# Reordering three groups of transfers in the loading queue of stage one

## The chip, the cores and the metric

The kernel runs on one core of a Trainium2 chip. The core has four engines that compute, each with its own instruction stream: PE (TensorE, matrix products into PSUM), DVE (VectorE), ACT (ScalarE) and POOL (GpSimd). A fifth, SP (SyncE), computes nothing here: it is the queue that issues nearly all transfers (DMAs), in program order. ACT issues a few of its own. An instruction that waits holds up everything behind it on the same engine. The metric is the time of one execution in microseconds of device time; lower is better.

## The reference

For `x` of 2048 tokens by 448 channels, the result mixes an attention branch `a` and an MLP branch `b` with a gate:

```python
g = sigmoid((x * gate_w).sum(-1, keepdims=True))
q = (x @ wq) in 16 heads of 28;  k = x @ wk;  v = x @ wv     # one k and v for all heads
a = softmax(q k^T * 28**-0.5) v @ wo
h = gelu(layernorm(x) @ w1)
hs = concat(h[0:112] shifted +1, h[112:224] -1, h[224:336] +2, h[336:448] -2) @ w2   # shifts along tokens
x1 = x + hs
b = x1 + gelu(layernorm(x1) @ w3) @ w4
out = g * a + (1 - g) * b
```

All data are fp32. The kernel splits each fp32 operand into a high and a low part and adds the products of high with high, high with low and low with high.

## The kernel before, in words

The tokens are cut in four blocks of 512, each of four tiles of 128. The order of the instructions on every engine is written out by hand, so program order is the order of each queue.

Stage one (to about 127 us of the profile) computes the projections of `x` and the token-shift half of the MLP branch:

- `stage_q(u)` computes one of 16 units (block by head group) of queries, keys, values and gate; ACT copies the result out of PSUM (L297) and issues its own store to the DRAM buffer `qd` (L298).
- `stage_kv(b)` reads block b's values back from `qd` as rows of the tile `vT` (two DMAs, L329). `stage_v` later transposes `vT` on PE (L350).
- `stage_w1(b)` computes `h` for block b, token tiles on partitions; DVE transposes it in 32 by 32 squares into `ht` (L436), and four DMAs (L439) store it to the DRAM buffer `hd`. `read_h(b)` reads it back with channels on partitions into `hr` (two DMAs, L447), which has to wait until the four stores have landed. These are the block's "channels".
- `split_h(b)` makes the high part on ACT (L461) and the low part on POOL, or for block 3 half of it on DVE (L463); then `carry_h(b)` sends four small DMAs (L409, L410), once the low part of the third group is there.
- `stage_w2(b)` multiplies by `w2` (PE, L477, L478, L480), 11 products for each of four token tiles. The PSUM tile `hs` has two buffers, so PE can start tile t+2 only when DVE has added tile t into `x1` (L482).
- The normalised `x1` of block 0 is the input of the second MLP half. `layernorm_norm` makes it on DVE (L159, L160), `xt_write(0)` stores it to the DRAM buffer `xd` (four DMAs, L167), `xt_read(0)` reads it back transposed into `xr` (three DMAs, L172, L174) once those stores have landed, and `ln_split` makes high and low parts (ACT L633, DVE L636, L638).
- `load_w34(i)` loads a pair of `w3` and `w4` chunks (L607, L608); `split_w3` and `split_w4` split them (ACT L106 to L109 and L614, DVE L113, L114 and L617).

Stage two (to about 402 us) runs `w3` and `w4` over the four blocks. Stage three is attention and the output.

The end of stage one, with what hangs on what: DVE does, in this order, the additions of block 1, the low parts of `split_h(3)`, the additions of block 2, `ln_split` of chunks 0 and 1, the first addition of block 3, `ln_split` of chunks 2 and 3, the split of `w3` chunk 0, the second addition, the split of `w4` chunk 0, and so on:

```python
def third(t):
    if t == 3:
        ln_split(0, 0, 2)
stage_w2(NB - 2, third)
def weights(t):
    if t == 0:
        ln_split(0, 2, 4)
    if t % 2 == 0:
        split_w3(t // 2)
    else:
        split_w4(t // 2)
        load_w34(t // 2 + 1, s2a)
```

So a late `xr` holds DVE, and with it the additions that PE waits for.

The loading queue from block 2 on, before the change: carries of block 1, `read_h(2)`, carries of block 2, the stores of `h` of block 3, `xt_write(0)`, `read_h(3)`, `stage_kv(0..2)`, carries of block 3, `load_w34(0)`, `xt_read(0)`, `stage_kv(3)`.

Of the kernel before, what the change touches and what calls it, by code (L numbers as in the profile page):

```python
# [42 lines left out]
def gated_mix_kernel(  # L43
# [85 lines left out]
    def proj(ps, wh, wl, ah, al):  # L129
        for c in range(3):  # L130
            nc.tensor.matmul(ps, wh[:, c, :], ah[:, c, :], start=(c == 0), stop=False)  # L131
            nc.tensor.matmul(ps, wh[:, c, :], al[:, c, :], start=False, stop=False)  # L132
            nc.tensor.matmul(ps, wl[:, c, :], ah[:, c, :], start=False, stop=False)  # L133
        nc.tensor.matmul(ps, wh[:, 3, :], ah[:, 3, :], start=False, stop=False)  # L134
        nc.tensor.matmul(ps, wl[:, 3, :], ah[:, 3, :], start=False, stop=True)  # L135
# [28 lines left out]
    def xt_write(b, xt4):  # L164
        xd_of[b] = dram.tile([NE, 32, 4, 128], F32, tag="xd", bufs=2, name=f"xd_{b}")
        for p in range(4):
            nc.sync.dma_start(xd_of[b][:, :, p].rearrange("f i u -> i f u"),  # L167
                              xt4[32 * p:32 * p + 32].rearrange("i f t j -> i f (t j)"))

    def xt_read(b, raw):  # L170
        xd = xd_of.pop(b)
        nc.sync.dma_start(raw[:, 0:3, :], xd[0:12].rearrange("(c f) i p u -> (f i) c (p u)", c=3))  # L172
        for k in (0, 64):
            nc.sync.dma_start(raw[k:k + 64, 3, :], xd[12:14].rearrange("f i p u -> (f i) (p u)"))  # L174
# [75 lines left out]
    with tc.tile_pool(name="s1b", bufs=1) as s1b, \  # L250
# [5 lines left out]
        def mm1(name):  # L256
            k = turn[0] % 4
            turn[0] += 1
            return mm_tile(name) if k < 2 else ps1.tile([P, 512], F32, tag="tp", bufs=2, name=name)
# [34 lines left out]
        def q_out(u, ps):  # L294
            b, g = divmod(u, NG)
            qf = s1.tile([P, 512], F32, tag="qf", bufs=4, name=f"qf_{u}")
            nc.scalar.copy(qf, ps)  # L297
            nc.scalar.dma_start(qd[g, :, 512 * b:512 * b + 512], qf)  # L298
# [13 lines left out]
        def stage_q(u, tile_of=mm1):  # L312
            b, g = divmod(u, NG)
            ps = tile_of(f"q_{u}")
            w = slice(g * P, (g + 1) * P)
            proj(ps, wqh[:, :, w], wql[:, :, w], *xact[b])
            q_out(u, ps)
# [4 lines left out]
        def rest(g, n, b):  # L322
            cols = slice(512 * b, 512 * b + 512)
            return qd[g].rearrange("(j c) s -> j c s", c=32)[0:n // 4, DH:32, cols]

        def stage_kv(b):
            for g in range(2):
                at = 32 * b + 16 * g
                nc.sync.dma_start(vT[at:at + 16, :], rest(2 + g, 16, b))  # L329
# [84 lines left out]
        def token_tile(b):  # L414
            ht = s1.tile([P, 4, 512], F32, tag="raw", bufs=3, name=f"ht_{b}").rearrange("p c n -> p (c n)")
            return ht[:, 0:4 * D].rearrange("p (f t j) -> p f t j", f=NE, t=4)

        def stage_w1(b, between=None, ht=None):
            ah, al = xact[b]
            rs = rs1_of.pop(b)[1]  # L420
            if ht is None:
                ht = token_tile(b)
            for t in range(4):
                ps = mm1(f"h_{b}_{t}")[:, 0:D]
                tok = slice(t * P, (t + 1) * P)
                for c in range(3):
                    nc.tensor.matmul(ps, ah[:, c, tok], w1h[:, c, :], start=(c == 0), stop=False)  # L427
                    nc.tensor.matmul(ps, al[:, c, tok], w1h[:, c, :], start=False, stop=False)  # L428
                    nc.tensor.matmul(ps, ah[:, c, tok], w1l[:, c, :], start=False, stop=False)  # L429
                nc.tensor.matmul(ps, ah[:, 3, tok], w1h[:, 3, :], start=False, stop=False)  # L430
                nc.tensor.matmul(ps, ah[:, 3, tok], w1l[:, 3, :], start=False, stop=True)
                hf = s1.tile([P, 512], F32, tag="hf", bufs=3, name=f"hf_{b}_{t}")[:, 0:D]
                nc.scalar.activation(hf, ps, AF.Gelu_apprx_tanh, scale=rs[:, t:t + 1])
                if between:
                    between(t)
                nc.vector.transpose(ht[:, :, t, :], hf.rearrange("p (f j) -> p f j", j=32))  # L436
            hd = hd_of[b] = dram.tile([NE, 32, 4, 128], F32, tag="hd", bufs=2, name=f"hd_{b}")
            for p in range(4):
                nc.sync.dma_start(hd[:, :, p].rearrange("f i u -> i f u"),  # L439
                                  ht[32 * p:32 * p + 32].rearrange("i f t j -> i f (t j)"))  # L440

        def read_h(b):
            hd = hd_of.pop(b)
            hr_of[b] = s1.tile([P, 4, 512], F32, tag="raw", bufs=3, name=f"hr_{b}")
            rows = hd.rearrange("f i p u -> (f i) (p u)").rearrange("(m c) n -> c m n", c=C)
            for m0, m1 in ((2, 4), (0, 2)):
                nc.sync.dma_start(hr_of[b][0:C, m0:m1, :], rows[:, m0:m1, :])  # L447

        def split_h(b):
            hh[b] = s1b.tile([P, 4, 516], F32R, tag="hh", bufs=2, name=f"hh_{b}")  # L450
            hl[b] = s1b.tile([P, 4, 516], F32R, tag="hl", bufs=2, name=f"hl_{b}")
            hr = hr_of.pop(b)
            for tt in (hl, hh):
                if b == 0:
                    nc.gpsimd.memset(f32(tt[b])[0:C, :, 0:2], 0.0)
                else:
                    nc.gpsimd.tensor_copy(tt[b][0:C, :, 0:2], f32(tt[b - 1])[0:C, :, 512:514])
            for m in ORDER:
                raw = hr[0:C, m, :].rearrange("n (p t j) -> n p t j", p=4, t=4)
                hi, lo = [tt[b][0:C, m, 2:514].rearrange("n (t p j) -> n p t j", p=4, t=4) for tt in (hh, hl)]  # L460
                nc.scalar.copy(hi, raw)  # L461
                eng = nc.vector if b == NB - 1 and m in (0, 3) else nc.gpsimd
                eng.tensor_tensor(lo, raw, f32(hi), ALU.subtract)  # L463
                if m == 2:
                    carry_h(b)
            for tt in (hh, hl):
                if b:
                    nc.gpsimd.tensor_copy(tt[b - 1][0:C, :, 514:516], f32(tt[b])[0:C, :, 2:4])
                if b == NB - 1:
                    nc.gpsimd.memset(f32(tt[b])[0:C, :, 514:516], 0.0)  # L470
# [83 lines left out]
        stage_w1(2, lambda t: ln1_tile(3, t))  # L554
        split_h(1)
        read_h(2)
        stage_q(12)
        stage_q(13)
        mv0, rs0 = stats_tiles(s1, "m")
# [9 lines left out]
        h3 = token_tile(3)  # L569
        xt4 = token_tile("x")  # L570
        stage_w1(3, fourth, h3)
        xt_write(0, xt4)
        read_h(3)
        for b in range(3):
            stage_kv(b)
        stage_w2(1)
        split_h(3)
        stage_q(14)
# [16 lines left out]
        def big(name):  # L595
            return s2a.tile([P, 2048], F32, tag="big", bufs=2, name=name)

        def load_w34(i, pool):
            w3h.append(pool.tile([P, 4, 2 * P], F32R, name=f"w3h_{i}"))
            w3l.append(pool.tile([P, 4, 2 * P], F32R, name=f"w3l_{i}"))  # L600
            last = late if 2 * i + 2 == NF else pool
            w4h.append(last.tile([P, 2, D], F32R, name=f"w4h_{i}"))
            w4l.append(last.tile([P, 2, D], F32R, name=f"w4l_{i}"))
            raw = big(f"w34raw_{i}")
            raw3[i] = raw[:, 0:1024].rearrange("p (c n) -> p c n", c=4)
            raw4[i] = raw[:, 1024:1024 + 2 * D].rearrange("p (c n) -> p c n", c=2)
            nc.sync.dma_start(raw3[i], w3[:, :, i * 256:i * 256 + 256])  # L607
            nc.sync.dma_start(raw4[i], w4[i * 256:i * 256 + 256, :].rearrange("(c p) n -> p c n", p=P))  # L608
# [10 lines left out]
        acts, xraw2 = {}, {}  # L619
# [18 lines left out]
                    nc.vector.tensor_sub(hi[64:128], raw[64:128], f32(hi)[64:128])  # L638

        xraw2[0] = big("xr_0").rearrange("p (c n) -> p c n", c=4)  # L640
        load_w34(0, s2a)
        xt_read(0, xraw2[0])
        stage_kv(3)

        def third(t):
# [551 lines left out]
```

## Time and profile before

| | us |
|---|---|
| median of 3 runs | 914.38 (913.28 to 914.83) |
| the profiled execution | 915.15 |
| its span in the trace | 913.4 |
| PE busy | 903.0 |
| DVE / ACT / POOL busy | 544.1 / 632.8 / 105.5 |

The span is what the instructions cover; 1.75 us of the profiled execution lie around it. Times "at 104.6" below are microseconds from the start of the span. In the views, `PE hs L477` is an instruction of PE that writes the tile `hs` on line 477; `SPq` is SP issuing a DMA; `DMA hr<-hd` is a transfer from `hd` to `hr` on its way. The chain of waits is the chain of work that ended last, followed back from the last instruction; each piece has its start and its length. A windows view gives the busy time of the engines, the number of instructions, the granted clock of PE (1.00 is full), the share of the 16 DMA engines that was busy and what they moved in GB/s.

### The profile page before, as it was taken

The numbers are of one execution on the slowest core, as the hardware profiler recorded it, in microseconds if no ns is written. First come the engines' busy times: TensorE is split into PE (matmuls) and PEld (weight loads), VectorE is DVE, ScalarE is ACT, GpSimd is POOL, SyncE is SP. The second block draws the span as 40 slices with busy tenths as digits, with TensorE's granted clock in tenths as the row PEclk, the third lists the DMA queues.
The fourth block names the chain that finished last, engine by engine and source line by source line (L and its number), as shares of the span: only waits on it lengthen the run. The fifth ranks groups of instructions, "written<-read, shape, count | busy, mean of one in ns | idle before, by whom it ended". The sixth has DMA issues, their size and how long they took to land.

```text
span 913.4 us, 24127 instructions
## 1 busy us (share of the span) xinstructions
PE 903.0 (99%) x10097; PEld 648.0 (71%) x10097; DVE 544.1 (60%) x1085; ACT 632.8 (69%) x1135; POOL 105.5 (12%) x138
## 2 busy tenths in 40 slices
PE   9999899999999999999999999999999999999997
PEld 7899778888888888875565565565656556666654
DVE  4656263631435736546666666676666667666675
ACT  5443154431231222159999999999999999999995
POOL 3134100212000340002200000000000000000000
PEclk9999999999999999999999999999999999999999
DMA  9875754130122142120000001101011000010001
GB/s 305 309 174 137 206 164 130 24 84 21 26 74 52 24 105 66 27 65 24 26 25 4 26 14 48 31 26 26 3 46 46 26 3 26 14 55 14 15 14 43
DMA packets 50368, 58.23 MB, mean 64 GB/s; under 512 B 9376, under 2 KB 34768, under 8 KB 50256
## 3 DMA queue, kind: packets, MB, share of 16 engines
q1 hardware_dynamic: 47088, 50.95, 20.2%
q10 hardware_dynamic: 3168, 5.70, 1.8%
q8 instruction: 80, 1.31, 0.6%
q14 instruction: 32, 0.26, 0.1%
HBM read 39.80 MB, written 15.59 MB: 61 GB/s over the span
## 4 chain that ended last, share of the span: by engine, by line
PE 94%; DMA 2%; DVE 1%; SPq 1%; ACT 1%; issue 0%; POOL 0%; DVEq 0%; POOLq 0%; ACTq 0%
PE bank L995 24%; PE bank L958 22%; PE bank L859 8%; PE acc L709 5%; PE acc L708 5%; PE acc L710 5%; PE g L132 4%; PE g L131 4%; PE g L133 4%; PE g L134 1%; PE g L135 1%; DMA xr<-xd 1%; PE h L427 1%; PE h L428 1%; PE h L429 1%; PE q L309 1%
## 5 line engine op out<-in xcount | busy, mean ns | idle before, releaser
L985 ACT ACTIVATE p<-bank 128x512 f32<-128x512 f32 x762 | 386.9, 615 | 2.1 <-PE bank L958 2.0
L995 PE MATMUL bank<-p,vext 128*32 128x256 f32 x3076 | 244.4, 379 | 0.0
L995 PE MATMUL bank<-pd,vext 128*32 128x256 f32 x1020 | 241.1, 379 | 0.0
L982 DVE COPY pd<-bank 128x512 f32<-128x512 f32 x254 | 175.2, 691 | 50.8 <-PE bank L958 49.1
L995 PEld LDWEIGHTS bank<-p,vext 128*32 128x32 f32 x3076 | 126.4, 110 | 82.2 <-ACT p L985 0.5
L697 ACT ACTIVATE gh<-g 128x512 fp32r<-128x512 f32 x54 | 32.3, 599 | 182.0 <-PE g L135 182.0
L999 DVE TENSOR_TENSOR o<-o,bank 128x256 f32<-128x256 f32 x222 | 93.5, 421 | 92.2 <-ACT p L985 54.0
L990 ACT ACTIVATE pd<-pd 128x1024 f32<-128x1024 f32 x127 | 140.4, 1106 | 0.0
L958 PE MATMUL bank<-qh,kH 30*128 30x512 f32 x1024 | 118.0, 443 | 0.0
L995 PEld LDWEIGHTS bank<-pd,vext 128*32 128x32 f32 x1020 | 111.8, 110 | 0.1
L700 DVE TENSOR_TENSOR gl<-gf,gh 128x512 fp32r<-128x512 f32 x54 | 37.2, 688 | 118.1 <-ACT gf L698 118.1
L958 PE MATMUL bank<-qh,kL 28*128 28x512 f32 x1024 | 105.4, 392 | 0.0
L958 PE MATMUL bank<-ql,kH 28*128 28x512 f32 x1024 | 105.0, 391 | 0.0
L958 PEld LDWEIGHTS bank<-qh,kH 30*128 30x128 f32 x1024 | 60.9, 182 | 57.5 <-ACT p L985 46.0
L709 PE MATMUL acc<-w4l,gh 128*128 128x448 f32 x216 | 78.9, 365 | 0.0
L708 PE MATMUL acc<-w4h,gh 128*128 128x448 f32 x216 | 78.8, 365 | 0.0
L710 PE MATMUL acc<-w4h,gl 128*128 128x448 f32 x216 | 78.7, 364 | 0.0
L859 PE MATMUL bank<-wof,on 128*32 128x224 f32 x1008 | 73.1, 367 | 0.0
L132 PE MATMUL g<-al,w3h 128*128 128x512 f32 x168 | 65.8, 392 | 0.0
L131 PE MATMUL g<-ah,w3h 128*128 128x512 f32 x168 | 65.6, 391 | 0.0
L133 PE MATMUL g<-ah,w3l 128*128 128x512 f32 x168 | 65.5, 390 | 0.0
L958 PEld LDWEIGHTS bank<-ql,kH 28*128 28x128 f32 x1024 | 52.0, 185 | 8.8
(203 smaller groups left out, 1165.9 us busy)
## 6 DMA issues: line engine op xcount, KB each, us to landing
qd<-qf ACTq DMA_DIRECT2D x16, 256.0 KB
qm<-qd SPq DMA_DIRECT2D x16, 256.0 KB
qr<-qd SPq DMA_DIRECT2D x16, 256.0 KB
rb<-rd SPq DMA_DIRECT2D x15, 256.0 KB
x<-in_x_dram SPq DMA_DIRECT2D x4, 896.0 KB
hd<-ht SPq DMA_DIRECT2D x16, 224.0 KB
hr<-hd SPq DMA_DIRECT2D x8, 448.0 KB
w34raw<-in_w_dram SPq DMA_DIRECT2D x7, 512.0 KB
```

Source lines behind the costliest of these rows:

```text
L131: nc.tensor.matmul(ps, wh[:, c, :], ah[:, c, :], start=(c == 0), stop=False)
L132: nc.tensor.matmul(ps, wh[:, c, :], al[:, c, :], start=False, stop=False)
L133: nc.tensor.matmul(ps, wl[:, c, :], ah[:, c, :], start=False, stop=False)
L708: nc.tensor.matmul(ps, gh[:, tok], w4h[i][:, k, :], start=(f == 0), stop=False)
L709: nc.tensor.matmul(ps, gh[:, tok], w4l[i][:, k, :], start=False, stop=False)
L710: nc.tensor.matmul(ps, gl[:, tok], w4h[i][:, k, :], start=False, stop=(f == stop))
L859: nc.tensor.matmul(ps[32 * j:32 * j + 32, cols], on_of[u][:, tok], wof[:, u % NG, cols], start=start, stop=stop, tile_position=(0, 32 * j))
L958: nc.tensor.matmul(bs[j], w, a, start=(i == 0), stop=(i == 2), tile_position=(32 * j, 0))
L982: nc.vector.tensor_copy(ps[j], bs[j])
L985: behind[kt % 2] = nc.scalar.activation(ps[j], bs[j], AF.Exp, scale=SCALE)
L990: ins = nc.scalar.activation(pd, pd, AF.Exp, scale=SCALE)
L995: nc.tensor.matmul(pv[32 * j:32 * j + 32, q], vext[:, kt, :], p_of[u, kt][j][:, q], start=start, stop=stop, tile_position=(0, 32 * j))
```

## The change

Three groups of DMAs change their place in SP's queue. `stage_kv(0..2)` goes from behind `read_h(3)` to behind `read_h(2)`; `read_h(3)` goes ahead of `xt_write(0)`; `xt_read(0)` goes ahead of `load_w34(0)`. No DMA and no instruction of another engine is added, removed or altered.

```diff
         stage_w1(2, lambda t: ln1_tile(3, t))
         split_h(1)
         read_h(2)
+        for b in range(3):
+            stage_kv(b)
         stage_q(12)
         stage_q(13)
...
         h3 = token_tile(3)
         xt4 = token_tile("x")
         stage_w1(3, fourth, h3)
+        read_h(3)
         xt_write(0, xt4)
-        read_h(3)
-        for b in range(3):
-            stage_kv(b)
         stage_w2(1)
         split_h(3)
...
         xraw2[0] = big("xr_0").rearrange("p (c n) -> p c n", c=4)
+        xt_read(0, xraw2[0])
         load_w34(0, s2a)
-        xt_read(0, xraw2[0])
         stage_kv(3)
```

## The prediction

> **What bounds the kernel now.** I read the page first (busy times and the chain's shares), then the waits of PE, then windows around them, then the chain of waits.
>
> ```profile
> PE 903.0 (99%) x10097; PEld 648.0 (71%) x10097; DVE 544.1 (60%) x1085; ACT 632.8 (69%) x1135; POOL 105.5 (12%) x138
> PE 94%; DMA 2%; DVE 1%; SPq 1%; ACT 1%; issue 0%; POOL 0%; DVEq 0%; POOLq 0%; ACTq 0%
> ```
>
> PE is the bound nearly throughout. What can be won lies where the chain leaves PE, and PE's waits say where that is:
>
> ```profile
> PE hs L477 <- DVE x L482: 4.2, 2, 2.3
> ```
>
> Two waits, together 4.2 us: PE wants a buffer of `hs` that DVE has not yet added into `x1`. Seven windows of PE, cut at these gaps (length, PE busy and count, granted clock, DMA share, GB/s):
>
> ```profile
> 100.29:104.58 4.29, 4.29 (x22) 1.00 0.57 153
> 104.58:107.30 2.72, 0.37 (x3) 1.00 0.32 78
> 107.30:110.77 3.47, 3.47 (x9) 0.51 0.82 247
> 110.77:117.75 6.98, 6.98 (x35) 1.00 0.85 257
> 117.75:120.00 2.25, 0.38 (x3) 1.00 0.00 0
> 120.00:124.56 4.56, 4.56 (x16) 0.63 0.37 89
> 124.56:126.63 2.07, 2.07 (x11) 1.00 1.04 331
> ```
>
> These 26.34 us are `stage_w2(2)` and `stage_w2(3)`. The fourth window gives the undisturbed pace: 34 products in 6.98 us (the 35th was under way at its start), 0.205 each, so 2.27 for the 11 of a token tile. Eight tiles need 18.1 us, plus four transposes of `vT`, 0.80 at the low clock in the chain below, so about 0.4: 18.5 us. **7.8 us are lost**: 2.5 in the first gap, 1.6 at clock 0.51 behind it (3.47 less 9 x 0.205), 2.0 in the second gap, 1.7 behind that. This is the most that the change can win. What sets the gaps stands in the chain:
>
> ```profile
> 88.56 0.31 SPq L439
> ...
> 91.62 1.22 SPq L167
> ...
> 96.80 0.30 SPq L447
> ...
> 97.16 6.62 DMA hr<-hd
> ...
> 105.98 3.02 DMA qd<-qf
> ...
> 109.02 0.40 SPq L608
> ...
> 109.46 7.97 DMA xr<-xd
> ...
> 117.46 0.63 ACT ah L633
> ...
> 119.33 0.62 DVE x L482
> ...
> 123.72 0.80 PE vp L350 x4
> ```
>
> First gap: the stores of `h` of block 3 (88.56), then the stores of `xd` (91.62), only then `read_h(3)` (96.80), which takes 6.6 us; DVE's half of `split_h(3)` waits for it, and the additions of block 2 stand behind that. Second gap: `xt_read(0)` goes out at 109.46, behind both loads of `load_w34(0)`, and takes 8.0 us; ACT splits at 117.46, DVE adds at 119.33, PE resumes at 120.00.
>
> **The change part by part.** Nothing is added, so each part is a question of when. First the **values' rows**:
>
> ```profile
> 75.38 1.68 SPq L447 DMA_DIRECT2D hr<-hd  x2
> 82.03 0.56 SPq L409 DMA_DIRECT2D hh<-hl  x1
> 98.30 4.68 SPq L329 DMA_DIRECT2D vT<-qd  x6
> vT<-qd SPq DMA_DIRECT2D x8, 32.0 KB
> ```
>
> The six issues take 4.7 us. In their new place SP is free from 77.06 to 82.03, 5.0 us, so the carries of block 2 start on time. Nor does a delay there cost anything at once: those carries take four times about 0.6, and SP has nothing more to do before 88.56. The six read `qd` of blocks 0 to 2, stored long before. A loss is possible if their 192 KB slow `hr` of block 2, which lands at about 81.5 and feeds block 3's `h`; they stand behind it in the queue, so I take 0, with 0.5 us as the other end.
>
> **Channels of block 3.** `read_h(3)` now stands right behind its own stores and must wait for them to land. Block 0 has that pattern:
>
> ```profile
> 46.76 3.09 SPq L439 DMA_DIRECT2D hd<-ht  x4
> 53.18 0.81 SPq L447 DMA_DIRECT2D hr<-hd  x2
> 57.08 0.63 ACT L461 CAST hh<-hr 112x512 fp32r<-112x512 f32 x1 [2.05 <-DMA hr<-hd]
> 58.37 1.68 ACT L461 CAST hh<-hr 112x512 fp32r<-112x512 f32 x3 [0.67 <-DMA hr<-hd]
> 102.48 0.62 ACT L461 CAST hh<-hr 112x512 fp32r<-112x512 f32 x1 [15.48 <-PE hs L478]
> 103.80 1.67 ACT L461 CAST hh<-hr 112x512 fp32r<-112x512 f32 x3 [0.69 <-DMA hr<-hd]
> 106.64 1.14 DVE L482 TENSOR_TENSOR x<-x,hs 128x448 f32<-128x448 f32 x2
> ```
>
> The read went out 6.42 us after the first store (46.76 to 53.18): here 88.56 + 6.42 = 94.98, against 96.80. The issue gains only 1.8 us, since SP now sits out the landing. But the read no longer shares the engines with `xd`'s stores: its halves were used 3.90 and 5.19 us after the issue in block 0, 5.68 and 7.00 in block 3. So 98.9 and 100.2, each 3.6 us earlier. (The row names PE for the wait at 102.48, but `stage_w2(1)` was done by 95.2; it was the transfer.) DVE's additions move from 106.64 to 103.0. PE wants the buffer at 104.8: the **first gap goes**, with 1.8 us to spare, and its slow stretch with it: 4.1 us. As far as that, the end has not moved, because the second gap would take it all back: PE would reach it 4.1 us sooner and wait for the same `xr`. The sum hangs on the landing of `xr`.
>
> **MLP input.** The stores of `xd` now start behind `read_h(3)`, 94.98 + 1.45 = 96.4, and take 4.6 us to issue as before (91.62 to 96.20), to 101.0; the carries of block 3 follow, to 103.5. `xr` may be read when the stores have landed:
>
> ```profile
> 178.84 3.05 SPq L167 DMA_DIRECT2D xd<-xt  x4
> 185.22 0.38 SPq L172 DMA_DIRECT2D xr<-xd  x1
> 190.63 2.19 ACT L633 CAST ah<-xr 128x512 fp32r<-128x512 f32 x4 [0.84 <-DMA xr<-xd]
> qd<-qf ACTq DMA_DIRECT2D x16, 256.0 KB
> ```
>
> In block 1 the read went out 6.38 us after the first store and 3.33 after the last issue. So 101.0 + 3.3 = 104.3 is the early end, and 100.2 + 6.4 = 106.6 the late one (stores that move only when `hr` is in). I take the middle, 105.5, against 109.46. The closed pool's last reader of `hr` (DVE, just ahead of the row of 106.64) moves to 103.0 and doesn't hold it. Block 1's `xr` was used 5.41 us after its issue, in an empty queue; 7.97 here, behind two weight loads. I take 5.41 + 0.6 for the two query stores of ACT, which go out at 102.4 and 103.4 (105.98 and about one us later, less 3.6) and should land by 105.4 and 106.4: `xr` is used at **111.5** instead of 117.46. The late end adds the whole of those 512 KB at the 257 GB/s of the fourth window, 2.0 us.
>
> The Trainium skill ("DMA: Bandwidth & Descriptors", section "Issuing engines are not separate DMA queues") says that transfers of SP and ACT run on the same 16 engines and interleave; by it the two stores share time with `xr` to the last byte, and the 2.0 of the late end would be nearer than my 0.6, which makes the sum 1.4 us smaller. No row here separates the two queues.
>
> **Weights behind it.** What is late next?
>
> ```profile
> w34raw<-in_w_dram SPq DMA_DIRECT2D x7, 512.0 KB
> 121.29 0.60 SPq L607 DMA_DIRECT2D w34raw<-in_w_dram  x1
> 119.55 0.83 ACT L106 CAST w3h<-w34raw 128x768 fp32r<-128x768 f32 x1
> 125.60 0.84 ACT L106 CAST w3h<-w34raw 128x768 fp32r<-128x768 f32 x1 [3.53 <-DMA w34raw<-in_w_dram]
> 122.64 0.61 DVE L482 TENSOR_TENSOR x<-x,hs 128x448 f32<-128x448 f32 x1
> ```
>
> The first `w3` load goes out at 105.5 + 2.1 = 107.6, and behind `xr` its 512 KB need 1.6 us at the 331 GB/s of the last window: 113.1. ACT gets to it 2.09 after `xr` (117.46 to 119.55): 113.6. So the weights just hide, with 0.5 us; if they land later, each us is one on the second addition. PE without gaps starts the third tile of block 3 at 100.29 + 6 x 2.27 = 113.9 and the fourth at 116.55. The first addition allows the third tile 2.54 us after `xr` (117.46 to 120.00), at 114.0; the second one ends 5.79 after it (123.25), at 117.3. So PE waits 0.1 and then about 0.65 more: **0.75 us remain**. `stage_kv(3)` lands behind the weights, some 1.4 us after them by the same rate, before the transposes at 116.2. The second weight pair goes out when DVE is done with `xr` (121.29, 3.83 after it): 115.3, used 4.31 later at 119.6. The gelus behind that are then ready before PE needs the first PSUM buffer again, two gate tiles of 2.5 us into stage two. From there to the end PE sets the pace, so what stage one gains the end gains.
>
> **Sum:** 7.8 less 0.75 is 7.05 us. On the profiled execution: 915.15 - 7.05 = 908.1; it lay 0.8 over the median, so in the runs 914.38 - 7.05 = **907.3 us**.
>
> One cost has no row: whether a short gap drops the clock. Gaps of 2.72 and 2.25 us each cost 1.6 behind them; smaller ones up to 0.75 don't occur here. I take 0, the other end is 1.6. The Trainium skill ("TensorE: Matmul & The Clock Gate", "Part 1") says that the clock halves after a whole idle window of about 3.4 us. By that, neither gap could have slowed PE and the change would be worth only the 4.5 us of gaps less 0.75: 910.6. The windows speak against it (0.51 and 0.63 granted), so it has no chance of its own below; the slow stretches of about 3.4 us do fit its window's length.
>
> **The rivals.**
>
> *`xr` comes later* (stores at their late end, 106.6; the read 5.71 as the slowest later block might have it; 2.0 for the query stores): 114.3. The third tile then starts at 116.85 instead of 113.9, a gap of 3.0 us, which drops the clock as now: the fourth follows 4.2 us later as it does now (120.00 to 124.2), at 121.1 instead of 116.55, and 0.1 of the slow stretch is behind it. 7.8 less 4.65 leaves 3.15 us: **911.2**. For it: SP waits longer in two places, the same engines carry it all, and waits of SP for the query stores are already on the chain (3.02 before L608). Against: the DMA share is only 0.32 and 0.57 in the first two windows, so there is room. Chance 0.20.
>
> *Nothing gained*: `xr` is set by the bytes ahead of it, not by its place; the first gap goes and comes back as a longer second one. That needs `xr` at about 117, 11.5 us after its issue. **914.4**. Against it: 8.0 was the time with two weight loads ahead. Chance 0.11. That the order in the queue changes and nothing else comes of it would be this case too.
>
> *Slower*: the weights, now behind a read that itself waits for stores, become the bound. PE's fourth tile can't start before ACT's `w3` split begins plus 3.7 (119.55 to 123.25). It started at 124.2 before; a loss of 1.8 us needs the split to begin at 122.3, 14.7 us after the load's issue at 107.6, where 4.31 was needed in the row of 121.29. At 124 the end would be at **917.9**. Chance 0.05.
>
> **How the numbers follow.** Forecast, 906 to 909: 0.64. With the three rivals that is 1. A measurement of this kernel tells about 0.2%, 1.8 us, from no change. Faster: 0.64 + 0.20 = 0.84; same 0.11; slower 0.05. The range: from 906.6 (all 7.8 won) less 0.8 of the runs' spread, 905.8, to the late rival, 911.3.
>
> **What would show it.** Right: L447 of block 3 issued at about 95 and ahead of L167; ACT's L461 at 99 and 100; no PE wait near 104.8 and the clock at 1.00 there; `xr` issued ahead of L607, at 105 to 106, ACT L633 at 111 to 112; the gate products of stage two starting at about 119.6 instead of 126.6, and the rest shifted by as much. Wrong: the six L329 pushing L409 of block 2 beyond 83; L633 beyond 114; ACT waiting for `w34raw` ahead of its first L106; PE waiting for `vT`; or PE's later stages growing by what was won.

## The result, and the profile after

| | before | changed |
|---|---|---|
| median, us | 914.61 (4 runs, 913.28 to 915.74) | 907.82 (4 runs, 907.61 to 908.86) |
| ratio, 95% interval | | 0.9929 (0.9911 to 0.9946) |
| profiled execution / its span | 915.15 / 913.4 | 907.61 / 905.8 |

The change wins 6.8 us, 0.7%, by the medians (the two profiled executions are 7.5 us apart, since the changed one is the fastest of its four). The page of the changed kernel, PE's busy time and the chain that ended last by engine:

```profile
PE 899.7 (99%) x10097; PEld 644.9 (71%) x10097; DVE 543.4 (60%) x1085; ACT 632.9 (70%) x1135; POOL 105.8 (12%) x138
PE 99%; ACT 0%; DVE 0%; issue 0%; ACTq 0%; DVEq 0%
```

The chain had left PE for 6% of the span; now PE carries 99% of it. PE itself is busy 3.3 us less, with the same 10097 instructions: the slow stretches are gone. All waits of PE in the changed kernel (us in total, times, longest):

```profile
PE warm_ps L93 <- DVE warm L66: 1.1, 1, 1.1
PE bank L1131 <- DVE worst L1127: 0.4, 1, 0.4
PE bank L902 <- ACT p L985: 0.3, 1, 0.3
```

The row of `hs` on L477 is gone. The windows of PE around the end of stage one, first of the changed kernel, then the last stretch of the kernel before (length, PE busy and count, granted clock, DMA share, GB/s):

```profile
100.55:118.88 18.33, 18.33 (x93) 1.00 0.79 231
118.88:905.80 786.92, 781.87 (x9548) 1.00 0.14 39
```
```profile
126.63:913.40 786.77, 781.68 (x9548) 1.00 0.14 39
```

`stage_w2(2)` and `stage_w2(3)` take 18.33 us without a gap, where they took 26.34. The gate products start at 118.88 instead of 126.63, 7.75 us earlier, and what follows takes 786.9 us as before. So the whole difference lies ahead of stage two, and nothing of it is given back behind. What SP issued, from the timeline of the changed kernel (start, length, issue):

```profile
77.19 4.21 SPq L329 DMA_DIRECT2D vT<-qd  x6
82.09 0.63 SPq L409 DMA_DIRECT2D hh<-hl  x1
...
87.81 3.02 SPq L439 DMA_DIRECT2D hd<-ht  x4
94.25 0.81 SPq L447 DMA_DIRECT2D hr<-hd  x2
95.11 3.83 SPq L167 DMA_DIRECT2D xd<-ht_x  x4
100.27 0.59 SPq L409 DMA_DIRECT2D hh<-hl  x1
...
104.81 0.39 SPq L172 DMA_DIRECT2D xr<-xd  x1
105.91 1.14 SPq L174 DMA_DIRECT2D xr<-xd  x2
107.09 0.60 SPq L607 DMA_DIRECT2D w34raw<-in_w_dram  x1
```

and who used it (the idle time ahead and what ended it stand in brackets):

```profile
98.44 0.63 ACT L461 CAST hh<-hr 112x512 fp32r<-112x512 f32 x1 [11.33 <-DMA hr<-hd]
99.78 1.67 ACT L461 CAST hh<-hr 112x512 fp32r<-112x512 f32 x3 [0.72 <-DMA hr<-hd]
110.03 2.18 ACT L633 CAST ah<-xr 128x512 fp32r<-128x512 f32 x4 [7.05 <-DMA xr<-xd]
112.66 0.83 ACT L106 CAST w3h<-w34raw 128x768 fp32r<-128x768 f32 x1 [0.45 <-DVE x L482]
```
```profile
102.83 0.62 DVE L482 TENSOR_TENSOR x<-x,hs 128x448 f32<-128x448 f32 x1
115.22 0.60 DVE L482 TENSOR_TENSOR x<-x,hs 128x448 f32<-128x448 f32 x1
```

`hr` is used 4 us earlier than before, `xr` 7.4 us earlier (117.46 then). The second fence is DVE's timeline: it adds block 2's first tile at 102.83, when PE has just made it, and block 3's second at 115.22, before PE wants the buffer at about 116.5. Last, SP's own waits that bear on this (us in total, times, longest):

```profile
SPq L447 <- DMA hd<-ht: 3.2, 1, 3.2
...
SPq L172 <- DMA qd<-qf: 0.9, 1, 0.9
SPq L174 <- DMA qd<-qf: 0.7, 1, 0.7
```

The first is `read_h(3)` sitting out the landing of its own stores. The other two are odd: `xr` doesn't read `qd`. They turned out to matter.

### The profile page after: what moved, and what is told of

It is laid out like the page before. It is cut to its first block, busy times and chain, and to the rows that moved or that the text cites. A ratio compares the mean times of both kernels' runs of the same rounds, so it can differ in the third digit from the quotient of the medians.

```text
span 905.8 us, 24129 instructions
## 1 busy us (share of the span) xinstructions
PE 899.7 (99%) x10097; PEld 644.9 (71%) x10097; DVE 543.4 (60%) x1085; ACT 632.9 (70%) x1135; POOL 105.8 (12%) x138
## 4 chain that ended last, share of the span: by engine, by line
PE 99%; ACT 0%; DVE 0%; issue 0%; ACTq 0%; DVEq 0%
PE bank L995 24%; PE bank L958 23%; PE bank L859 8%; PE acc L709 5%; PE acc L708 5%; PE acc L710 5%; PE g L132 4%; PE g L131 4%; PE g L133 4%; PE hs L477 1%; PE hs L478 1%; PE g L134 1%; PE g L135 1%; PE hs L480 1%; PE h L429 1%; PE h L427 1%
```

## The experiments

The theory on trial: the two gaps are in series, and the end of stage one is set by the landing of `xr`. The rival: each of the three parts takes its own gap, independently. Three parts give eight kernels; with those before and after, six runs fill the table.

**The channels alone.**

```diff
         stage_w1(3, fourth, h3)
+        read_h(3)
         xt_write(0, xt4)
-        read_h(3)
         for b in range(3):
             stage_kv(b)
```

> Only read_h(3) goes ahead of xt_write(0); the values' rows and the order of xr and weights stay as before. Theory (two gaps in series, the end set by the landing of xr): the first gap goes, but the six L329 now stand between xd's stores and block 3's carries, so SP comes to load_w34(0) at about 106.6 and to xr at about 107.9; behind the weights xr takes 8.0 and ACT L633 starts at about 115.9. PE waits 4.5 us ahead of block 3's third tile and runs slow behind it: about 1.7 us faster than before, 912.9. Rival (two independent gaps, each part takes its own): 4.1 us faster, 910.5, with the second gap as long as before.

Measured: 917.32 (12 runs) against 914.81, ratio 1.0026 (1.0017 to 1.0034). It is *slower* than before, where both theories had a gain. From this run, in order: the timeline of SP, the waits of SP, the timeline of ACT, the waits of PE:

```profile
100.39 7.88 SPq L329 DMA_DIRECT2D vT<-qd  x6
108.39 0.63 SPq L409 DMA_DIRECT2D hh<-hl  x1
```
```profile
SPq L329 <- DMA qd<-qf: 2.9, 1, 2.9
```
```profile
118.94 2.18 ACT L633 CAST ah<-xr 128x512 fp32r<-128x512 f32 x4 [14.49 <-DMA xr<-xd]
```
```profile
PE hs L477 <- DVE x L482: 5.6, 1, 5.6
```

The first gap is gone: one wait on L477 is left. But the six rows take 7.9 us instead of the 4.7 they took before, since SP waits 2.9 us for a store of queries to land, which the rows of blocks 0 to 2 don't read. All behind them is late: the carries, the weights, and `xr`, used at 118.94, later than before. The second gap takes back all that the first gave, and more. PE also waits 0.6 and 0.2 us for the late carries near 111. That the second gap takes back the first holds; the forecast of 1.7 us gained was a miss in its sign too, since the theory knew nothing of that wait.

**The MLP input alone.**

```diff
+        xt_read(0, xraw2[0])
         load_w34(0, s2a)
-        xt_read(0, xraw2[0])
         stage_kv(3)
```

> Only xt_read(0) goes ahead of load_w34(0). Theory: the first gap stays (2.5 us and 1.6 us of low clock near 105 to 111), xr goes out at 107 to 109 and is used at 112.5 to 114.5, and PE, late by the first gap, finds DVE's additions done: no second gap, about 3.6 us faster than before, 911.0. Rival (independent gaps) gives the same 3.7 here; the two differ in e1.

Measured: 911.63 (6 runs), ratio 0.9961 (0.9947 to 0.9974). The time is as expected, and the one gap left is the first (`[1.90 <-DVE x L482]` on PE's L477 at 107.56). `xr` goes out at 107.68, as expected too, but is used 0.8 us after the latest time that I had given. It takes 7.65 us with no weight load ahead of it. What stands ahead of it are ACT's two query stores, by ACT's timeline:

```profile
106.23 0.34 ACTq L298 DMA_DIRECT2D qd<-qf  x1
...
107.28 0.34 ACTq L298 DMA_DIRECT2D qd<-qf  x1
115.33 2.19 ACT L633 CAST ah<-xr 128x512 fp32r<-128x512 f32 x4 [8.07 <-DMA xr<-xd]
```

**The values' rows alone.**

```diff
         read_h(2)
+        for b in range(3):
+            stage_kv(b)
...
         read_h(3)
-        for b in range(3):
-            stage_kv(b)
```

> Only the values' rows move. Theory: nothing waits for them, the carries of block 3 wait for POOL and not for SP, both gaps stay: within 0.3 us of before, 914.5. Rival (the six transfers are in the way of hr or xr by their traffic): up to 1 us faster. If they disturb block 2's channels in their new place: up to 0.5 us slower, L409 of block 2 issued after 82.5.

Measured: 915.07 (12 runs), ratio 1.0001 (0.9992 to 1.0009): nothing, as expected. L409 of block 2 went out at 82.33. PE's two waits are still there on its timeline:

```profile
106.51 0.47 PE L477 MATMUL hs<-w2h,hh 112*128 112x448 f32 x1 [1.20 <-DVE x L482]
119.94 0.74 PE L477 MATMUL hs<-w2h,hh 112*128 112x448 f32 x1 [4.12 <-DVE x L482]
```

This run shows the series most plainly. In its profiled execution the first gap is half as long as before (1.20 against 2.35), and the second has grown from 1.87 to 4.12, since `xr` is used at 117.41 as ever.

**Channels and input, rows left where they were.**

```diff
         stage_w1(3, fourth, h3)
+        read_h(3)
         xt_write(0, xt4)
-        read_h(3)
         for b in range(3):
             stage_kv(b)
...
+        xt_read(0, xraw2[0])
         load_w34(0, s2a)
-        xt_read(0, xraw2[0])
```

> The change without the move of the values' rows. Theory: both gaps shrink, but the six L329 hold SP until about 104, so block 3's carries and xr go out 2 to 3 us later than in the changed kernel (xr at about 106.6 instead of 104.8), L633 starts at about 112, the second addition of block 3 ends about 1.2 us too late for PE: about 6.5 us faster than before, 908.1 to 909, so the rows' move is worth 0.5 to 1.3 us here though it is worth nothing alone. Rival (the rows' move is worth nothing anywhere): 907.8, as the changed kernel.

Measured: 913.52 (12 runs), ratio 0.9979 (0.9968 to 0.9990). A miss: without the rows' move only 0.2% is left of the 0.7%. The same wait as in the first run is why (SP's timeline, then SP's waits):

```profile
99.45 7.84 SPq L329 DMA_DIRECT2D vT<-qd  x6
107.42 0.63 SPq L409 DMA_DIRECT2D hh<-hl  x1
...
110.14 0.52 SPq L172 DMA_DIRECT2D xr<-xd  x1
```
```profile
SPq L329 <- DMA qd<-qf: 3.1, 2, 2.8
```

The chain of waits has it too: `104.16 2.50 DMA qd<-qf`, then `106.67 0.63 SPq L329`. So `xr` goes out 5.3 us later than in the changed kernel (104.81).

In the program as compiled, the DMAs of SP and ACT take eight completion counters in turn, and each waits until the DMA that had its counter before it, eight earlier in the program's count, has landed. The two query stores of block 3 are issued by ACT behind `split_h(3)`, which itself waits for `hr`; with the channels moved, their counters fall to the fifth and sixth of the rows when these stand where they stood, and to the first two reads of `xr` in the changed kernel: the odd waits above. In the kernel before they fall to the second weight load and to the last read of `xr`, and SP's waits there show both:

```profile
SPq L608 <- DMA qd<-qf: 1.3, 1, 1.3
...
SPq L174 <- DMA qd<-qf: 0.6, 1, 0.6
```

The order of the counters is read off the program; the next run tries it.

**The same with the last two query stores issued by SP.**

```diff
-            nc.scalar.dma_start(qd[g, :, 512 * b:512 * b + 512], qf)
+            (nc.sync if u > 13 else nc.scalar).dma_start(qd[g, :, 512 * b:512 * b + 512], qf)
```

> As the run with channels and input alone (rows still between xd's stores and block 3's carries), but the last two query stores are issued by SP behind the carries instead of by ACT. Theory (a DMA must wait until the one eight before it in the program's count of DMAs, those of ACT included, has landed; so the sixth row waited for a query store): now the row's predecessor is a store of xd, landed by then, the wait of 2.8 us goes, and although SP issues two more DMAs, xr goes out at about 108 instead of 110.1: 1 to 3.5 us faster than that run, 910 to 912.3. Rival (the time is SP's issuing alone): 1.2 us slower than that run, about 914.7.

Measured: 912.12 (10 runs), ratio 0.9962 (0.9947 to 0.9977). The timelines of SP and of ACT:

```profile
99.86 4.19 SPq L329 DMA_DIRECT2D vT<-qd  x6
104.17 0.63 SPq L409 DMA_DIRECT2D hh<-hl  x1
...
107.98 0.39 SPq L172 DMA_DIRECT2D xr<-xd  x1
```
```profile
114.66 2.18 ACT L633 CAST ah<-xr 128x512 fp32r<-128x512 f32 x4 [11.35 <-DMA xr<-xd]
```

The rows take 4.2 us again, and `xr` goes out at 107.98 although SP issues two more DMAs. They read the same data as in the run before, and the wait of 2.8 us is gone, as the counters had it: it belongs to them and not to the data. In time it brings little: the query stores now stand in the same queue just ahead of `xr`, which is used 6.7 us after its issue (5.1 in the run before), so only 0.6 us of the 2.2 arrive. The intervals of the two runs overlap.

**The rows behind the weights**, the other way to take SP past that wait.

```diff
         xt_read(0, xraw2[0])
         load_w34(0, s2a)
+        for b in range(3):
+            stage_kv(b)
         stage_kv(3)
```

> The values' rows of all four blocks go behind load_w34(0) instead of ahead. Theory (what the move of the rows bought is that SP no longer stands between xd's stores and block 3's carries, where its sixth row waited 2.8 us for a query store): the late place is as good as the early one, xr at about 104.8 as in the changed kernel, PE waits at most 0.5 us for vT: 907.8 to 908.5. Rival (the early place itself matters, since the rows' traffic is then out of the way): 909 to 910.

Measured: 908.47 (6 runs), ratio 0.9923 (0.9909 to 0.9936), the changed kernel's value. So it is not the early place that pays: the late one, clear of the stretch between the stores of `xd` and block 3's carries as well, is worth the same. In its profile `xr` went out at 107.42 and not at 104.8, because the stores of `h` started late in it (90.36); counted from them it is 17.1 us, against 17.0 in the changed kernel. The price of the late place showed where it was expected, though longer, among the waits of PE:

```profile
PE vp L350 <- DMA vT<-qd: 1.6, 1, 1.6
```

**Channels and rows, weights still ahead of the input.**

```diff
         xraw2[0] = big("xr_0").rearrange("p (c n) -> p c n", c=4)
-        xt_read(0, xraw2[0])
         load_w34(0, s2a)
+        xt_read(0, xraw2[0])
```

(against the changed kernel)

> The change without its third part: read_h(3) ahead of xt_write(0), values' rows behind read_h(2), but load_w34(0) still ahead of xt_read(0). Theory: no first gap; SP reaches the weights at about 104.8 and xr at about 106.5, and behind the weights xr takes 6.5 to 8.0, so L633 starts at 113 to 114.5 and PE waits 1.6 to 3 us ahead of block 3's third tile: 910 to 911.6, half the gain. Rival (the weights ahead of xr cost nothing once SP is early): 907.8.

Measured: 913.52 (11 runs, 910.51 to 914.27), ratio 0.9972 (0.9960 to 0.9983). The profiled execution, at 911.53, is as expected: `xr` issued at 107.09, used at 114.06, one gap of 2.6 us. The median is 2 us worse than I had said. Ahead of the weights `xr` took 5.2 us in the changed kernel, behind them 7.0 here: both its place and its time in flight count.

**Rows and input, channels behind the stores of `xd`.**

```diff
+        xt_write(0, xt4)
         read_h(3)
-        xt_write(0, xt4)
```

(against the changed kernel)

> Rows and MLP input moved, channels of block 3 still behind xd's stores. Theory: the first gap stays (1.2 to 2.5 us, with the low clock behind it if it is over 1.6 or so), xr goes out at 107 to 108 and is used near 113 to 115, PE is late enough not to wait for it again: as the run with the input alone, 911 to 912. Rival (two of three parts bring two thirds): 910.

Measured: 912.18 (8 runs), ratio 0.9970 (0.9960 to 0.9981): as the run with the input alone, and as the theory had it. The first gap is there, 2.6 us at 107.78, and no second.

**The weights 1.45 us later.**

```diff
         xt_read(0, xraw2[0])
-        load_w34(0, s2a)
         stage_kv(3)
+        load_w34(0, s2a)
```

> The changed kernel with stage_kv(3) ahead of load_w34(0), so the first weights go out 1.45 us later. Theory: they had some 0.7 us to spare behind xr, so PE waits 0 to 0.5 us ahead of block 3's fourth tile, too short to lower the clock (a gap of 1.2 us in the run with the rows alone did not): 907.8 to 908.4. Rival (the weights set the end already): each us counts, 909.2.

Measured: 908.19 (6 runs), ratio 0.9919 (0.9905 to 0.9932); no loss that can be told. Its profiled execution is its slowest (910.05; the stores of `h` went out at 89.12 in it, 1.3 us after those in the changed kernel's profile) and shows two short gaps on PE's timeline:

```profile
114.82 0.47 PE L477 MATMUL hs<-w2h,hh 112*128 112x448 f32 x1 [0.65 <-DVE x L482]
118.50 0.47 PE L477 MATMUL hs<-w2h,hh 112*128 112x448 f32 x1 [0.72 <-DVE x L482]
```

**The changed kernel once more**, unaltered.

> The changed kernel once more, unaltered, for a second profiled execution. Theory: what is left over is thin. If the stores of h of block 3 start at 88.6 or later (they started at 87.81 in the first profile of it, at 88.6 to 90.4 in others), the weights or xr hold PE 0.3 to 1 us, without a drop of the clock; if they start before 88, not at all. Time 907.5 to 908.9 either way. Rival (the first profile is typical): no PE wait on L482 at all.

Measured: 908.52 (5 runs), ratio 0.9927 (0.9912 to 0.9942). The stores of `h` started at 88.76 in this profile, and PE did wait a little, by its timeline:

```profile
117.09 0.47 PE L477 MATMUL hs<-w2h,hh 112*128 112x448 f32 x1 [0.35 <-DVE x L482]
```

So the first profile, with no wait at all, was a favourable execution. The change leaves some tenths of a microsecond of slack, not more.

All eight together (ratio to the kernel before, measured beside each):

| | rows not moved | rows moved |
|---|---|---|
| nothing else | 1 | 1.0001 |
| channels | 1.0026 | 0.9972 |
| input | 0.9961 | 0.9970 |
| channels and input | 0.9979 | 0.9929, 0.9927 |

The rival is dead: channels alone lose, rows alone do nothing, and adding the singles' gains (0.26% lost, 0.39% and 0.0% won) gives 0.1%, not 0.7%. Taken out of the whole, each part costs about as much as the next: the rows 0.50%, the input 0.43%, the channels 0.41%, which the intervals don't tell apart.

## Why the prediction was right, and where it was off

907.3 us was forecast, 907.82 measured; the gain of 7.05 came out as 6.8.

- **The two gaps and their slow stretches as all there is to win**: right. The two `stage_w2` lost 8.0 us of their 26.34 (to 18.33), 7.8 forecast.
- **`read_h(3)` ahead of the stores**: right in kind and size. It went out 6.44 us after the first store of `h` (6.42 forecast), and its halves were used 4.2 and 5.5 us after that (3.9 and 5.2). The stores themselves started 0.75 us earlier than in the profile before, which the change doesn't explain (see the last section).
- **The landing of `xr` decides**: right, and shown by the runs with the rows alone and with the channels alone, where the first gap shrank or went and the second one grew.
- **When `xr` may go out**: the number came out, the reason did not. I let it wait for the stores of `xd` until 105.5, 16.9 us after the first store of `h`; it went out at 104.81, 17.0 us after it. But four windows of the changed kernel (length, busy time of PE, PEld, DVE, ACT and POOL, clock, DMA share, GB/s) show those stores done by about 102:

```profile
99.00:100.00 1.00, 1.00 (x6) 0.81 (x5) 0.00 (x0) 0.28 (x2) 0.86 (x1) 1.00 1.14 341
100.00:101.00 1.00, 1.00 (x6) 0.88 (x5) 0.50 (x1) 1.00 (x3) 0.24 (x1) 1.00 1.15 345
101.00:102.00 1.00, 1.00 (x6) 0.94 (x5) 0.70 (x2) 0.93 (x2) 0.99 (x1) 1.00 0.86 251
102.00:103.00 1.00, 1.00 (x6) 0.92 (x6) 0.88 (x2) 0.59 (x1) 0.96 (x5) 1.00 0.27 86
```

  What `xr` waited for, 0.9 us, was ACT's query store, by way of the counter. That the time fitted is luck: a wait that I had not understood stood in for one that was not there. I had seen SP's waits for query stores in the profile before, and had priced them without asking why a load that doesn't read `qd` should wait for it.
- **The query stores' cost to `xr`**: 0.6 us allowed; `xr` was used 5.22 us after its issue, 0.2 less than in the empty queue of block 1. The page "DMA: Bandwidth & Descriptors" of the Trainium skill (section "Issuing engines are not separate DMA queues") would have had them interleave; here they had landed before the second read of `xr` went out, so this run can't speak for or against. The runs with the input alone and with rows and input agree with the Trainium skill there: ACT's stores went out up to 1.5 us ahead of `xr`, and it took 7.65 and 6.2 us. With the stores on SP, just ahead of `xr` in its own queue, it took 6.7. Beside such stores 0.6 is too little, though block 3's carries move in the same stretch and their share is not told apart.
- **The weights just hide**: nearly. ACT was ready for them at 112.2 and had them at 112.66, so it did wait, which I had listed as a sign of being wrong. (The row names DVE's addition, but in the run with the rows last the same wait, 0.41 us, is put down to the load, and the program has L106 wait for no addition.) DVE, busy with `xr` to 113.83, lost nothing by it, and the run with the weights later shows no loss that can be told.
- **The values' rows at no cost and no worth**: the step that was wrong. Alone they are worth nothing (1.0001). With the channels moved they are worth 0.5%, about 4.6 us (0.9979 to 0.9929 with the input, 1.0026 to 0.9972 without), because in their old place they then hold SP twice: by a wait that comes into being with the channels' move, and by the 4.2 us of their own issuing. Counted from the first store of `h`, block 3's carries go out after 18.7 us with channels and input alone, after 15.4 without the wait (stores on SP), and after 12.5 in the changed kernel, which waits for the same query stores with its carries already out. How the 4.6 us divide is not shown: taking away the wait alone brought about 1.5 us (0.9979 to 0.9962), with intervals that overlap and with the query stores ahead of `xr` in its queue. I had asked what waits for the rows, and not what the rows wait for in their old place once everything around them moves.
- **The residue of 0.75 us**: none in one profile, 0.35 in the other. Where a gap is that short the clock holds; the 0 I took was right.
- **The rivals**: none of them came. What a late `xr` costs can be seen in the run with channels and rows: used at 114.06, where the rival had 114.3, it was profiled at 911.53, near the rival's 911.2 (its median is 913.52).

## What to carry to other kernels

When two stalls are in series, find the event that ends last and price every edit by what it does to that event: removing the first alone can lose time, as here. When transfers change their place in a queue, list for each what it waits for in the new order, counters shared with other queues among them; a wait for data that an instruction doesn't read is the sign of one. And run the parts of a compound change apart: the part that did nothing alone was worth as much as either of the others once all three stood together.

## What the runs showed of the hardware that was not expected

**How short a gap lowers PE's clock.** Gaps of 0.35, 0.65, 0.72, 1.20 and 1.61 us (the runs of the changed kernel again, weights later, rows alone, rows last) left the clock at 1.00 behind them; those of 1.90, 2.58, 2.61 and 2.92 us (input alone, channels and rows, rows and input, channels and input), and the 1.87 and 2.35 of the kernel before (PE's idle time in the prediction's windows of 2.25 and 2.72 us), were followed by a clock of 0.50 for about 3.4 us; those of 3.20, 4.12 and 5.62 us (stores on SP, rows alone, channels alone) had about twice that, part of it inside the gap. The Trainium skill ("TensorE: Matmul & The Clock Gate", "Part 1") asks for a whole idle window of 3.4 us; here 1.87 us was enough and 1.61 was not. Each length was seen once, so a fixed limit between the two is not shown. Two windows (length, PE busy and count, granted clock, DMA share, GB/s), one behind the gap of 1.61 (rows last) and one behind that of 1.90 (input alone):

```profile
121.00:122.00 1.00, 1.00 (x6) 1.00 1.05 365
```
```profile
110.00:111.00 1.00, 1.00 (x4) 0.50 1.08 291
```

**One DVE instruction, two lengths.** The third normalisation of block 0, on the path to the stores of `h`, first in the kernel before, then in the changed one:

```profile
84.29 1.43 DVE L159 TENSOR_SCALAR xn<-x,mv_s_m,rs_s_m 128x448 f32<-128x448 f32 x1
```
```profile
84.17 0.61 DVE L159 TENSOR_SCALAR xn<-x,mv_s_m,rs_s_m 128x448 f32<-128x448 f32 x1
```

It took 1.1 to 1.4 us in all runs but this one and the rows alone (0.55). POOL works on L463 beside it in both of these profiles. Why it was short in two was not tried; the 0.82 us between the two rows is about what the stores of `h` started earlier by in the first profile of the changed kernel: at 87.81, against 88.56 in the kernel before and 88.76 in the second profile.

**Stores alone and beside a read.** Two windows of the kernel before, in the columns of the four windows of the changed kernel above, while the stores of `h` were in flight:

```profile
90.00:91.00 1.00, 1.00 (x7) 0.92 (x6) 0.10 (x1) 0.00 (x0) 0.00 (x0) 1.00 1.00 175
91.00:92.00 1.00, 1.00 (x7) 0.92 (x6) 0.53 (x1) 0.00 (x0) 0.00 (x0) 1.00 0.95 159
```

Here they moved at 159 to 175 GB/s, and in the changed kernel, alone from 89 to 93, at 173 to 215. Those of `xd`, issued behind `read_h(3)`, moved beside it at 251 to 345 GB/s for both together, and all was in by about 102, so `xr` was not held by them. The windows don't part the two, so whether the stores themselves went faster beside the read is not shown.
